# Causal scores and values in 64x64 quarters of TensorE's array, with the masked quarter left out

## The chip, the core and the metric

One core of a Trainium2 chip runs the whole program. A core has TensorE (PE, matmuls, which writes to the banks of PSUM), VectorE (DVE), ScalarE (ACT), GpSimd (POOL), and SyncE (SP), which here issues most loads. Each engine works through its own instructions in order and waits on semaphores for the others. The metric is the time of one execution on the device in microseconds (us); lower is better. Before the change it is 606.27 us, the median of three runs (605.86 to 606.37).

## What is computed

A retention layer (linear attention with a decay `gamma` for each head, causal), then a gated feed-forward layer without an activation, then a normalised one with SiLU. All of it is in float32:

```python
def _attn_ref(q, k, v):                       # 2 batches, 8 heads, 768 steps, 64 wide
    gamma = 1.0 - 2.0 ** (-5.0 - np.arange(H))
    for t in range(S):
        state = gamma * state + np.einsum('bhd,bhe->bhde', k[:, :, t], v[:, :, t])
        y[:, :, t] = scale * np.einsum('bhd,bhde->bhe', q[:, :, t], state)

x = y as 1536 tokens x 512
x = ((x @ w_a) * (x @ w_b)) @ w_out                       # 512 -> 1536 -> 512
xn = x / sqrt(mean(x * x) + 1e-6) * rms_g
out = (silu(xn @ w_gate) * (xn @ w_val)) @ w_out2         # 512 -> 1536 -> 512
```

## The kernel before

**Stages.** The retention layer fills the first 70 us, the two feed-forward layers the rest. The change is in the retention layer alone, which is worked in 12 chunks of 128 steps (6 per batch; chunk n and n + 2 are neighbours of one batch). The 8 heads of a chunk are 4 pairs `p` of 2 heads `r`; the 64 numbers of head `r` lie in the lower or upper 64 partitions. For every chunk there are four PE steps. `scores` (tile `sc`): keys times queries, 8 matmuls with 64 rows in, 128 out and 128 columns; DVE multiplies the two banks by the decayed causal mask, which gives `p`. `past` (tile `ya`, from `sd` and `qd`): queries times the state from earlier chunks, 8 matmuls of 64 by 64 and 128 columns, each in a quarter of the 128x128 array; chunks 0 and 1 have none. `values` (tile `ya`, from `p` and `k`): values times masked scores, 8 matmuls of 128 by 64 and 128 columns, added to the same banks. `state` (tile `st`, from `vd`): 8 matmuls of 128 by 64 and 64 columns; the last two chunks have none. In the trace each float32 matmul of the retention layer is two instructions, so a step of 8 matmuls is 16 rows.

**Around them.** `vd` (values times a decay) is made on DVE or POOL, `qd` (queries times a decay) on POOL or DVE, `sd` (the state) is copied out by ACT. After `values` ACT rounds the result to `xh`, DVE forms the rest `xl`, and ACT copies it once more to `xf` or `x`. The first products of the feed-forward layer (`c`, three passes with `xh`, `xl` and the weights `uh`, `ul`) are mixed in between the chunks. Loads go through SP: per chunk a queries-and-keys tile (512 KB, named `q`) and a keys-and-values tile (512 KB, named `k`), the mask (512 KB), weights (`raw`, 512 KB each).

**Order.** Nothing is issued in the order of the code. `Plan` records every operation; `dues` and `list` (lines 355 to 470) sort them with priced durations, and the table `SHIFTS` moves single operations earlier or later. The string `HEAD` (line 83) says in which order the steps of the retention stage are recorded: S scores, P past, V values, T state, `d` the decays, `m` the mask load, and `warm8` for 8 matmuls on zeros ahead of all. Every PE matmul goes through `mm` (line 536), which gives its price to the plan; every instruction is emitted by line 492, so the trace tells groups apart by tile names.

## Time and profile before

| what | value |
|---|---|
| median of three runs | 606.27 us |
| the profiled execution | 605.8 us, of which the profile's span is 604.0 us |
| PE busy | 595.6 us (99%) |
| DVE, ACT, POOL busy | 489.1 (81%), 422.4 (70%), 118.9 us (20%) |
| retention stage | from the first `sc` at 6.72 us to the first `y` at 69.77 us |
| granted clock of PE | 1.00 nearly throughout; 0.50 from 8.49 to 15.32 us |

A granted clock of 1.00 is 2.4 GHz, 0.50 is 1.2 GHz. A row of the timeline gives start and length of a run of alike instructions; the length reaches to the modelled end of the last one and so past the start of the next, because matmuls are pipelined. What a run costs the engine is therefore read from its start to the next run's start.

### The profile page before, as it was taken

The page shows a single profiled execution, that of the slowest core. Times are in us where ns is not written, and L with a number is a line of the kernel's source. Part 1 is how long each engine was busy: PE and PEld are TensorE (multiplying, and loading weights), DVE is VectorE, ACT ScalarE, POOL GpSimd, SP SyncE. Part 2 cuts the span into 40 slices and gives each one's busy share as a digit, 9 for nine tenths or more (in the row PEclk, how much of TensorE's full clock was granted, in tenths as well). Part 3 has the DMA queues.
Part 4 walks back from the last instruction along what each step waited for, and adds up shares of the span by engine and source line. Part 5 has one row for each costly group of instructions (what it writes and reads, how often), then busy time and mean ns, then how long its engine had stood idle before and what let it go on. Part 6 is the DMA issues. An engine that isn't in the chain of part 4 may idle for free.

```text
span 604.0 us, 9800 instructions
## 1 busy us (share of the span) xinstructions
PE 595.6 (99%) x3584; PEld 509.7 (84%) x3584; DVE 489.1 (81%) x886; ACT 422.4 (70%) x804; POOL 118.9 (20%) x135
## 2 busy tenths in 40 slices
PE   7999999999999999999999999999999999999997
PEld 6988888988888888888897888888888888888886
DVE  4799796695898996887789999598888898698554
ACT  5756787455888886778556977588687897787630
POOL 1330000013223323323100000002242323233210
PEclk7999999999999999999999999999999999999999
DMA  8884146018979988799941134335897897878875
GB/s 327 303 321 174 43 151 227 2 45 140 246 144 200 206 160 169 148 174 171 279 152 35 37 138 154 125 78 121 168 191 141 160 195 163 164 146 155 135 214 206
DMA packets 40352, 98.27 MB, mean 163 GB/s; under 512 B 4590, under 2 KB 4974, under 8 KB 40304
## 3 DMA queue, kind: packets, MB, share of 16 engines
q0 software_dynamic: 17312, 31.47, 35.4%
q1 hardware_dynamic: 22704, 66.07, 32.3%
q8 instruction: 28, 0.46, 0.3%
q10 hardware_dynamic: 288, 0.10, 0.1%
q14 instruction: 20, 0.16, 0.1%
HBM read 56.73 MB, written 40.89 MB: 162 GB/s over the span
## 4 chain that ended last, share of the span: by engine, by line
PE 91%; DMA 3%; issue 2%; DVE 2%; POOL 1%; ACT 0%; SPq 0%; POOLq 0%; DVEq 0%
PE b L492 30%; PE y L492 17%; PE d L492 16%; PE x_P L492 12%; PE c L492 11%; PE ya L492 2%; PE sc L492 2%; DMA q<-in_qk 1%; DMA acc<-out 1%; DMA out<-z 1%; PE st L492 1%; POOL out L492 1%; DVE vd L492 1%; PE ms L492 0%; PE rb L492 0%
## 5 line engine op out<-in xcount | busy, mean ns | idle before, releaser
L492 POOL DMA_DIRECT2D out<-z x60 | 52.4, 900 | 229.1 <-ACT z L492 197.9
L492 POOL DMA_DIRECT2D partial<-z x60 | 52.4, 926 | 204.9 <-ACT z L492 174.1
L492 PE MATMUL y<-h,o 128*128 128x512 f32 (+2 forms) x294 | 69.8, 389 | 1.2 <-DVE h L492 0.7
L492 PEld LDWEIGHTS y<-h,o 128*128 128x128 f32 x294 | 53.9, 188 | 13.2 <-DVE h L492 1.0
L492 ACT COPY z<-x_P 128x512 f32<-128x512 f32 x88 | 50.8, 589 | 18.3 <-PE x_P L492 16.6
L492 PE MATMUL b<-xh,uh 128*128 128x512 f32 x160 | 62.8, 392 | 0.0
L492 PE MATMUL b<-xl,uh 128*128 128x512 f32 x160 | 62.6, 391 | 0.0
L492 PE MATMUL b<-xh,ul 128*128 128x512 f32 x160 | 62.4, 390 | 0.0
L492 DVE TENSOR_TENSOR ul<-wt,uh 128x512 fp32r<-128x512 f32 x82 | 53.6, 686 | 6.1 <-ACT uh L492 6.0
L492 ACT CAST uh<-wt 128x512 fp32r<-128x512 f32 x82 | 48.3, 622 | 12.0 <-PE d L492 9.7
L492 ACT CAST v<-raw 128x512 f16<-128x512 bf16 x72 | 56.0, 791 | 0.5
L492 PE MATMUL x_P<-r,l 128*128 128x512 f32 x192 | 51.9, 391 | 0.0
L492 ACT ACTIVATE v<-raw 128x512 int32<-128x512 uint32 x72 | 48.2, 679 | 3.6 <-DMA raw<-in_w 3.6
L492 PE MATMUL y<-h,l 128*128 128x512 f32 x192 | 47.6, 390 | 0.0
L492 PE MATMUL b<-th,uh 128*128 128x512 f32 x120 | 47.2, 394 | 0.0
L492 PE MATMUL b<-tl,uh 128*128 128x512 f32 x120 | 47.1, 392 | 0.0
L492 PE MATMUL b<-th,ul 128*128 128x512 f32 x120 | 46.7, 389 | 0.0
L492 DVE TENSOR_TENSOR u<-u,b 128x512 f32<-128x512 f32 x40 | 27.4, 685 | 23.7 <-PE b L492 16.8
L492 ACT COPY z<-y 128x512 f32<-128x512 f32 x56 | 32.8, 587 | 18.8 <-PE y L492 16.9
L492 DVE TENSOR_TENSOR g<-g,d 128x256 f32<-128x256 f32 x80 | 33.3, 418 | 15.3 <-ACT g L492 7.9
L492 PE MATMUL d<-xh,ul 128*128 128x256 f32 x160 | 45.2, 283 | 0.0
L492 PE MATMUL d<-xl,uh 128*128 128x256 f32 x160 | 45.2, 283 | 0.0
(148 smaller groups left out, 1512.6 us busy)
## 6 DMA issues: line engine op xcount, KB each, us to landing
raw<-in_w SPq DMA_DIRECT2D x72, 512.0 KB, 4.8
partial<-z POOLq DMA_DIRECT2D x60, 256.0 KB, 5.3
out<-z POOLq DMA_DIRECT2D x60, 256.0 KB, 5.1
q<-in_qk SPq DMA_DIRECT2D x12, 512.0 KB, 6.7
k<-in_kv SPq DMA_DIRECT2D x10, 512.0 KB, 7.9
partial<-z SPq DMA_DIRECT2D x12, 256.0 KB, 2.1
acc<-partial SPq DMA_DIRECT2D x6, 512.0 KB, 6.8
out<-z SPq DMA_DIRECT2D x12, 256.0 KB, 2.8
```

What stands on the lines that cost most here:

```text
L492: getattr(self.engines[op.engine], method)(real(out), *map(real, args), **{k: real(a) for k, a in kwargs.items()})
```

## The change

Of a 128 x 128 block of scores the quarter of the later keys and the earlier queries is masked to zero. The new kernel does not compute it.

- **`scores`**: 16 matmuls instead of 8, each 64 rows by 64 outputs, in a quarter of the array: the earlier 64 keys against all 128 queries (128 columns), the later 64 keys against the later 64 queries (64 columns). For every second pair of heads the two key halves change places on the partitions (`turned`, on the host), so that of two pairs one fills each half of the bank with 128 columns and the other with 64. The bank holds 384 instead of 512 columns.
- **mask**: packed to the same 384 columns per bank; its load is 384 KB instead of 512 KB, and the DVE product `p` runs over 128x384 instead of 128x512.
- **`values`** is cut in two. A new step `early` takes the earlier queries: 8 matmuls of 64 by 64 and 64 columns. The rest takes the later queries: 8 matmuls of 128 by 64 and 64 columns.
- **marks**: `early` reads other rows of the array than `past` and adds to the same outputs. After `past` of each of the 10 chunks that have one, ACT copies 64x1 of the bank to `marks`, and one matmul of a single column reads that copy ahead of `early` (against the zero tile `warm`, into an unused column).
- `warm8` becomes `warm13`, the price in `mm` for a 64x64 matmul now grows with its columns, and `SHIFTS` holds other numbers, so the order of other work changes too.

```diff
-    6: -96050, 8: 11700, 17: 7750, 19: 24150, 22: 17850, 39: 18750, 40: 26200, 45: 18750, 58: -35200, 64: -17850, 95: 19200, 98: 26400, 113: 2800,
...
+    5: -64750, 6: -71600, 7: -68050, 19: 21550, 22: 20500, 30: 36800, 41: 16750, 45: 18750, 46: 15900, 62: -37200, 72: 5700, 76: 2000, 101: 20400,
...
-HEAD = "lq0 lw m lk0 warm8 S0 d L1 lq3 lq2 lk2 x c0 x x lw lk3 x W0 P0 V0 F0 x w1 S1 Q2 L4 x T0 lw lw P1 V1 F1 T1 x x Ha0 S2 P2 V2 F2 Q3 w2 c0 S3 x T2 W3 P3 x x V3 F3 x S4 x T3 L5 L6 D2 Q4 W4 L7 c1 Ua0 x Q5 W5 T4 x Hb0 Ub0 x D3 G0 S5 P4 V4 R0 F4 x L8 Q6 W6 x S6 T5 P5 V5 F5 c1 x L9 Q7 w7 x T6 S7 P6 V6 F6 x L10 D4 Q8 W8 P7 T7 V7 F7 S8 x x L11 q9 W9 x t0 t1 c1 x x Ua1 Ub1 G1 x x S9 P8 R1 x D5 T8 q10 V8 F8 x t1 c1 Ua2 x x Ub2 x G2 x R2 S10 P9 V9 F9 x q11 t1 T9 x Ua3 x x Ub3 G3 S11 x R3 T10 P10 P11 V10 F10 x x t1 V11 F11"
+HEAD = "lq0 lw m lk0 warm13 S0 d L1 lq3 lq2 lk2 x c0 x x lw lk3 x W0 P0 V0 F0 x w1 S1 Q2 L4 x T0 lw lw P1 V1 F1 T1 x x Ha0 S2 P2 V2 F2 Q3 w2 c0 S3 x T2 W3 P3 x x V3 F3 x S4 x T3 L5 L6 D2 Q4 W4 L7 c1 Ua0 x Q5 W5 T4 x Hb0 Ub0 x D3 G0 S5 P4 V4 R0 F4 x L8 Q6 W6 x S6 T5 P5 V5 F5 c1 x L9 Q7 w7 x T6 S7 P6 V6 F6 x L10 D4 Q8 W8 P7 T7 V7 F7 S8 x x L11 q9 W9 x t0 t1 c1 x x Ua1 Ub1 G1 x x S9 P8 R1 x D5 T8 q10 V8 F8 x t1 c1 Ua2 x x Ub2 x G2 x R2 S10 P9 V9 F9 x q11 t1 T9 x Ua3 x x Ub3 G3 S11 x R3 T10 P10 P11 V10 F10 x x t1 V11 F11"
...
-        n = out.shape[-1]
+        n = 1
+        for size in out.shape[1:]:
+            n *= size
...
-        each = 0.443 * n if n > HB else 123.6 if n == HB else 111 if full else 111 * (n + 8) / 136 if out.shape[0] == P or a[0].shape[0] == P else 54
+        each = 0.443 * n if n > HB else 123.6 if n == HB else 111 if full else 111 * (n + 8) / 136 if out.shape[0] == P or a[0].shape[0] == P else 54.6 * (n + 8) / 136
...
-            mask_sb = ac.tile([P, 2, NP, C], F32, name="mask_sb")
+            mask_sb = ac.tile([P, 2, NP // 2, 3, C // 2], F32, name="mask_sb")
+            warm = ac.tile([P, P], F32, name="warm")
...
-                p_t[n] = a2.tile([P, 2, NP, C], F32, tag="p", name=f"p{n}")
-                sc = [bank("Y", f"sc{n}_{r}").rearrange("p (n c) -> p n c", n=NP) for r in range(2)]
+                p_t[n] = a2.tile([P, 2, NP // 2, 3, C // 2], F32, tag="p", name=f"p{n}")
+                sc = [bank("Y", f"sc{n}_{r}")[:, :NP // 2 * 3 * C // 2].rearrange("p (e x c) -> p e x c", e=NP // 2, x=3) for r in range(2)]
                 plan.cut()
+                q, k = (qk_t[n][:, e].rearrange("p n (x c) -> p n x c", x=2) for e in range(2))
                 for p in range(NP):
-                    for r in range(2):
-                        h = slice(r * D, (r + 1) * D)
-                        mm(sc[r][:, p, :], qk_t[n][h, 1, p, :], qk_t[n][h, 0, p, :], start=True, stop=True)
+                    for first in (1, 0):
+                        for r in range(2):
+                            h = slice(r * D, (r + 1) * D)
+                            if first:
+                                to, x = p & 1, slice(0, 2 + (p & 1), 1 + (p & 1))
+                            else:
+                                to, x = 1 - (p & 1), slice(1 + (p & 1), 2 + (p & 1))
+                            mm(sc[r][to * D:(to + 1) * D, p // 2, x], k[h, p, 1 - first], q[h, p, 1 - first:], start=True, stop=True)
...
+            ya_all = {}
+            marks = ac.tile([P, LINE // 8], F32, name="marks")
+
             def past(n):
-                ya_t[n] = [bank(tag, f"ya{n}_{r}").rearrange("p (n c) -> p n c", n=NP)[:, :NP // 2] for r, tag in enumerate(("A", "AY"[n % 2]))]
+                ya_all[n] = [bank(tag, f"ya{n}_{r}") for r, tag in enumerate(("A", "AY"[n % 2]))]
+                ya_t[n] = [y.rearrange("p (n c) -> p n c", n=NP)[:, :NP // 2] for y in ya_all[n]]
...
+                    plan.cut()
+                    act.copy(marks[:D, n:n + 1], ya_t[n][1][:D, 1, C - 1:])
+
+            def early(n):
+                plan.cut()
+                if n >= B:
+                    mm(ya_all[n][0][:D, NP // 2 * C:NP // 2 * C + 1], warm[:D, :D], marks[:D, n:n + 1], start=False, stop=True, skip_group_check=True)
+                for p in range(NP):
+                    for r in range(2):
+                        to, e = place(p, r)
+                        h = slice((p & 1) * D, (1 + (p & 1)) * D)
+                        mm(ya_t[n][r][to, e, :C // 2], kv_t[n][h, 1, 2 * p + r, :], p_t[n][h, r, e, 0, :], start=(n < B), stop=True, skip_group_check=True)
 
             def values(n):
+                early(n)
                 j, o = n // CPT, (n % CPT) * C
                 if o == 0:
                     x_tiles(0, j)
                     if j < 2:
                         xf[j] = [held(place_of("sum", 2 * j + r), [P, 2, TB], F32, f"xf{j}_{r}") for r in range(2)]
-                y = ya_t.pop(n)
+                y = ya_t[n]
                 plan.cut()
                 for r in range(2):
                     for p in range(NP):
                         to, e = place(p, r)
-                        mm(y[r][to, e, :], kv_t[n][:, 1, 2 * p + r, :],
-                           p_t[n][:, r, p, :], start=(n < B), stop=True, skip_group_check=True)
+                        mm(y[r][to, e, C // 2:], kv_t[n][:, 1, 2 * p + r, :],
+                           p_t[n][:, r, e, 1 + (p & 1), :], start=(n < B), stop=True, skip_group_check=True)
...
+def turned(a, axis, heads):
+    a = a.copy()
+    for h in range(H):
+        if h // 2 % 2:
+            one = (slice(None),) * heads + (h,)
+            a[one] = a[one].take([*range(C // 2, C), *range(C // 2)], axis=axis - (heads < axis))
+    return a
...
-    mask = mask.reshape(NP, 2, C, C).transpose(2, 1, 0, 3).reshape(C, 2 * NP * C)
+    mask = turned(mask, 1, 0).reshape(NP // 2, 2, 2, C, 2, C // 2).transpose(3, 2, 0, 1, 4, 5)
+    mask = np.stack([np.concatenate([mask[r * C // 2:(r + 1) * C // 2, :, :, r, :1], mask[r * C // 2:(r + 1) * C // 2, :, :, :, 1]], axis=3) for r in range(2)])
+    mask = mask.reshape(C, 2 * (NP // 2) * 3 * (C // 2))
...
-    kv = np.stack([i[n].reshape(B, H, CPB, C, D).transpose(2, 0, 3, 1, 4).reshape(NCH, C, DM) for n in ("k", "v")], axis=2).reshape(NCH, C, 2 * DM)
+    kv = [i[n].reshape(B, H, CPB, C, D).transpose(2, 0, 3, 1, 4) for n in ("k", "v")]
+    kv = np.stack([turned(a, 2, 3).reshape(NCH, C, DM) for a in kv], axis=2).reshape(NCH, C, 2 * DM)
```

**PE, third and fourth chunk.** Before: the end of `past` of one chunk (tile `ya_0_290`), `values` of both, `st` and the next `sc`.

```order
L492 MATMUL ya_1_292<-qd_256,sd_237 64x128
L492 MATMUL ya_0_277<-p_270,k_221 64x128 x4
L492 MATMUL ya_1_279<-p_270,k_221 64x128 x4
L492 MATMUL ya_0_290<-p_287,k_239 64x128 x4
L492 MATMUL ya_1_292<-p_287,k_239 64x128 x4
L492 MATMUL st<-vd_309,k_221 64x64 x8
L492 MATMUL sc_0_340<-q_258 128x128
```

The same place after: the last two of `early` for the third chunk, `st`, the rest of its `values`, `st` of the next chunk, and the first `sc` of the fifth.

```order
L489 MATMUL ya_0_330<-p_325,k_176 64x64
L489 MATMUL ya_1_332<-p_325,k_176 64x64
L489 MATMUL st<-vd_327,k_176 64x64 x8
L489 MATMUL ya_0_330<-p_325,k_176 64x64 x4
L489 MATMUL ya_1_332<-p_325,k_176 64x64 x4
L489 MATMUL st<-vd_350,k_198 64x64 x8
L489 MATMUL sc_0_404<-q_216 64x128
L489 MATMUL sc_1_406<-q_216 64x128
L489 MATMUL sc_0_404<-q_216 64x64
L489 MATMUL sc_1_406<-q_216 64x64
```

What moved: the two `values` no longer stand together; each has 8 matmuls of `early` ahead of it, and the fourth chunk's comes behind the fifth chunk's scores.

**ACT, the same place.** After, with the two marks (`ya_1_332` and `ya_1_342` are the banks of the third and fourth chunk); PE's matmul on the first mark stands directly behind the fourth chunk's `past`.

```order
L489 COPY g_305<-c_0_0_266 128x256
L489 COPY marks<-ya_1_332 64x1
L489 COPY marks<-ya_1_342 64x1
L489 COPY sd_384<-st 128x256
L489 CAST xh_0_196<-ya_0_330 128x2x128
L489 ACTIVATE v_1_402<-raw_1_247 128x512
```

Before, the conversion of a weight (`v`) stood directly between `g` and the `xh` of the third chunk:

```order
L492 COPY g_254<-c_0_0_224 128x256
L492 ACTIVATE v_1_274<-raw_1_205 128x512
L492 CAST v_1_274<-raw_1_205 128x512
L492 CAST xh_0_172<-ya_0_277 128x2x128
L492 CAST xh_0_172<-ya_1_279 128x2x128
```

Here the marks and one copy of the state now come ahead of it, and the weight's conversion comes behind the first `xh`.

**SP, the first loads.** Before:

```order
L492 DMA raw_0_84<-in_w 128x1024
L492 DMA q_97<-in_qk 128x1024
L492 DMA mask_sb<-in_mask 128x1024
L492 DMA q_102<-in_qk 128x1024
L492 DMA k_104<-in_kv 128x1024
L492 DMA k_106<-in_kv 128x1024
L492 DMA q_108<-in_qk 128x1024
L492 DMA q_132<-in_qk 128x1024
L492 DMA raw_1_205<-in_w 128x1024
```

After:

```order
L489 DMA raw_0_84<-in_w 128x1024
L489 DMA q_102<-in_qk 128x1024
L489 DMA mask_sb<-in_mask 128x768
L489 DMA k_107<-in_kv 128x1024
L489 DMA q_109<-in_qk 128x1024
L489 DMA k_111<-in_kv 128x1024
L489 DMA q_113<-in_qk 128x1024
L489 DMA q_145<-in_qk 128x1024
L489 DMA k_176<-in_kv 128x1024
```

The first values tile now comes ahead of the second queries tile (on PE the first chunk's `values` now stands ahead of the second chunk's `sc`), and the second weight moved from the ninth to the twelfth load.

## Rows read from the trace of the kernel before

**Rows 1.** The page: the span, busy times, and the granted clock in 40 slices.

```profile
span 604.0 us, 9800 instructions
PE 595.6 (99%) x3584; PEld 509.7 (84%) x3584; DVE 489.1 (81%) x886; ACT 422.4 (70%) x804; POOL 118.9 (20%) x135
PEclk7999999999999999999999999999999999999999
```

**Rows 2.** Busy by stretch: PE, PEld, DVE, ACT, POOL; granted clock, DMA share, GB/s.

```profile
5.08:8.49 3.41, 1.76 (x18) 1.26 (x18) 1.54 (x3) 2.05 (x3) 0.00 (x0) 1.00 1.03 421
8.49:15.32 6.83, 6.47 (x58) 5.09 (x58) 4.85 (x8) 4.35 (x13) 1.85 (x2) 0.50 1.02 411
32.40:36.00 3.60, 2.84 (x62) 2.19 (x50) 3.60 (x6) 1.46 (x5) 2.98 (x2) 1.00 0.92 328
17.97:69.77 51.80, 51.04 (x717) 44.29 (x716) 45.26 (x76) 31.35 (x77) 8.76 (x7) 1.00 0.57 211
```

**Rows 3.** Timeline of PE at the start: start, length, run, [idle before, releaser].

```profile
1.06 3.78 PE L492 MATMUL w<-warm 128*128 128x128 f32 x16 [1.06 <-DVE small L492]
6.72 1.16 PE L492 MATMUL sc<-q 64*128 64x128 f32 x16 [1.88 <-DMA q<-in_qk]
7.82 1.43 PE L492 MATMUL decays<-tables 2*128 2x512 f32 x2
9.30 2.08 PE L492 MATMUL sc<-q 64*128 64x128 f32 x16
```

**Rows 4.** Timeline of DVE and POOL at the start: who waits for which load.

```profile
8.06 1.29 DVE L492 TENSOR_TENSOR p<-sc,mask_sb 128x512 f32<-128x512 f32 x2 [0.46 <-DMA mask_sb<-in_mask]
11.95 1.04 POOL L492 TENSOR_TENSOR vd<-k,dg_sb 128x512 f32<-128x512 f32 x1 [9.97 <-DMA k<-in_kv]
14.51 2.52 POOL L492 TENSOR_TENSOR qd<-q,dq_sb 128x512 f32<-128x512 f32 x2 [1.52 <-DMA q<-in_qk]
```

**Rows 5.** Timeline of PE, retention steps of later chunks, at full clock.

```profile
17.97 2.06 PE L492 MATMUL sc<-q 64*128 64x128 f32 x32
19.95 1.10 PE L492 MATMUL ya<-qd,sd 64*64 64x128 f32 x32
20.99 1.97 PE L492 MATMUL ya<-p,k 128*64 128x128 f32 x32
22.79 0.63 PE L492 MATMUL st<-vd,k 128*64 128x64 f32 x16
23.35 1.16 PE L492 MATMUL sc<-q 64*128 64x128 f32 x16
24.44 0.69 PE L492 MATMUL st<-vd,k 128*64 128x64 f32 x16
...
40.74 0.64 PE L492 MATMUL st<-vd,k 128*64 128x64 f32 x16
41.21 1.05 PE L492 MATMUL ya<-p,k 128*64 128x128 f32 x16
...
48.47 0.67 PE L492 MATMUL ya<-qd,sd 64*64 64x128 f32 x16
49.06 0.69 PE L492 MATMUL st<-vd,k 128*64 128x64 f32 x16
```

**Rows 6.** Timeline of DVE and PE around 35 us.

```profile
32.55 1.77 DVE L492 TENSOR_TENSOR vd<-k,dg_sb 128x512 f32<-128x512 f32 x1
34.98 0.66 PE L492 MATMUL ya<-p,k 128*64 128x128 f32 x8 [0.41 <-DVE p L492]
```

**Rows 7.** DVE groups from 17.97 to 69.77 us: count, busy, mean ns, idle before.

```profile
L492 DVE TENSOR_TENSOR p<-sc,mask_sb 128x512 f32<-128x512 f32 x20 | 13.0, 682 | 3.2 <-PE sc L492 3.2
L492 DVE TENSOR_TENSOR xl<-ya,xh 128x256 fp32r<-128x256 f32 x18 | 7.1, 414 | 0.8 <-ACT xh L492 0.8
```

**Rows 8.** Timeline of ACT: an operation on 128x2, and one step of the conversion of a weight.

```profile
2.47 0.20 ACT L492 ACTIVATE small<-small 128x2 f32<-128x2 f32 x1
...
19.05 0.77 ACT L492 CAST v<-raw 128x512 f16<-128x512 bf16 x1
```

More of the change, by code (lines that the diff above doesn't have):

```diff
@@ L1508, in gated @@
                 cast(0, *FIRST[i], g_t[i])
-            warm = ac.tile([P, P], F32, name="warm")
             vec.memset(warm, 0.0)
@@ L1517, in masks @@
             def masks(_):
-                dma("sp", mask_sb.rearrange("p r n c -> p (r n c)"), mask)
+                dma("sp", mask_sb.rearrange("p r e x c -> p (r e x c)"), mask)
             def decays(_):
@@ L1634, in _consts @@
     mask = np.where(apart >= 0, scale * g[:, None, None] ** np.maximum(apart, 0), 0)
-    mask = mask.reshape(NP, 2, C, C).transpose(2, 1, 0, 3).reshape(C, 2 * NP * C)
+    mask = turned(mask, 1, 0).reshape(NP // 2, 2, 2, C, 2, C // 2).transpose(3, 2, 0, 1, 4, 5)
+    mask = np.stack([np.concatenate([mask[r * C // 2:(r + 1) * C // 2, :, :, r, :1], mask[r * C // 2:(r + 1) * C // 2, :, :, :, 1]], axis=3) for r in range(2)])
+    mask = mask.reshape(C, 2 * (NP // 2) * 3 * (C // 2))
     c = np.arange(CPB)[:, None] * C
-    dk = g ** (S // 2 - (c + t)[:, :, None]).transpose(1, 0, 2)
+    dk = turned(g ** (S // 2 - (c + t)[:, :, None]).transpose(1, 0, 2), 0, 2)
     gq = np.repeat((g ** (c - C)).reshape(CPB, NP, 2, 1), D, axis=3).reshape(CPB, NP, P).transpose(2, 0, 1)
```

25 rows, old and new, of the table SHIFTS are left out of this document.

## The prediction

> **What bounds the kernel now.** I read the busy shares first: PE is busy for 595.6 of 604.0 us, DVE for 81%, the others for less [rows 1]. So time is lost or won on PE, and only in the retention stage, since nothing else is rewritten. There, from 17.97 to 69.77 us, PE is busy for 51.04 of 51.80 us and DVE for 45.26 [rows 2]: PE is the bound, DVE close behind. Before 17.97 us it is otherwise. PE starts its first scores at 6.72 us, after 1.88 us without work [rows 3]. Loads land one after the other: first queries 6.72, mask 8.06, second queries 9.30, the second values tile is waited for until 11.95, later queries until 14.51 [rows 3, 4], which is about 1.3 us for each 512 KB. And from 8.49 to 15.32 us PE is granted a clock of 0.50, the lower level of 1.2 GHz, after a stretch in which it was busy for 1.76 of 3.41 us [rows 2].
>
> **Prices of the PE steps**, at full clock, from start to start [rows 5]. Two chunks of scores take 19.95 - 17.97 = 1.98 us, one chunk 24.44 - 23.35 = 1.09: a chunk costs 0.89, coming from another array shape 0.20. `past`: two chunks 20.99 - 19.95 = 1.04, one chunk 49.06 - 48.47 = 0.59: 0.45 and 0.14 to 0.16. `values`: 22.79 - 20.99 = 1.80 for two, 0.90 each. `state`, which has the shape of `values` and half its columns, stands between two `values` from 40.74 to 41.21: 0.47. So on 128x64 half the columns cost half. And `past` shows that 64x64 matmuls with 128 columns run four at a time, at half the price of 128x64 (0.45 against 0.90).
>
> **Part 1, scores.** 8 matmuls of 128 columns in quarters, as `past`: 0.45. 8 more with 64 columns: 0.23 if a quarter also takes half the time for half the columns, 0.45 if it does not. I take 0.23, nearest to the 0.47 of `state`. New price 0.68, gain 0.89 - 0.68 = 0.21 a chunk; other bound -0.01, no gain.
>
> **Part 2, values.** The later queries have the shape of `state`: 0.47. `early`, 8 matmuls of 64x64 and 64 columns: 0.23, bound 0.45. Sum 0.70 (0.92), gain 0.20 (bound -0.02). For the 10 chunks behind 17.97 us both parts give 10 x 0.41 = 4.1 us, or nothing.
>
> **Part 3, changes of shape.** Behind 17.97 us there are now 7 stretches of 64x128, 6 of 64x64, 7 of 128x64 and 4 of full arrays; by the order after the change 10 of 64x64, 9 of 128x64 and 6 full. At 0.20, 0.16, 0.20 (`state` alone lasts 0.69 from 24.44 on, less 0.47 [rows 5]) and 0.19 for full arrays, an estimate from the other three, that is 1.4 + 0.96 + 1.4 + 0.76 = 4.5 us before and 1.6 + 1.8 + 1.14 = 4.5 after. Zero.
>
> **Part 4, marks.** Ten matmuls of one column, two instructions each, stand ahead of `early`. No row shows one; the smallest step of 16 costs 0.47, so 0.03 an instruction, and because the next matmul of that quarter waits for both I take 0.1 us, 1.0 in all. Each also waits for an ACT copy of 64x1, and all of PE is queued behind it. The smallest ACT operation took 0.20 us [rows 8]. In two places (chunks 2 and 6, counted from 0) only one `past` of 0.45 us lies between the copied result and the mark; result, copy and signal need more, so some 0.3 us of waiting each, 0.6 together. In the other eight, scores, `values` or `y` lie between, at least 0.7 us, which hide a copy unless ACT has other work ahead of it. Sum +1.6 us; bounds +0.3 (waits hidden) and +9 (rival 3).
>
> **Part 5, DVE.** The 20 products `p` from 17.97 on take 682 ns for 512 columns, `xl` 414 for 256 [rows 7]; 384 should take 548, so DVE loses 20 x 0.134 = 2.7 us of its 45.26. PE's stretch shrinks by as much as 3, so DVE's share stays where it is, near 88%, and waits for it stay possible. Now there is one: around 35 us PE waits for a `p` that stood behind a `vd` of 1.77 us, which ran beside POOL's `qd` [rows 6]; in that stretch PE was idle for 0.76 of 3.60 us [rows 2]. DVE has other neighbours in the new order; I take half of it back, -0.4 us (bounds -0.8 and +1.2), and +0.5 for new waits on DVE (0 to +1.5). ACT's ten copies, 2 us on an engine busy for 31.35 of 51.80 [rows 2], cost only through the marks.
>
> **Part 6, the start.** The mask is 128 KB smaller: a quarter of 1.3 us, it lands near 7.7 instead of 8.06. Then come first values (9.0), second queries (10.3), second values (11.6), later queries (12.9, 14.2). The order after: first scores 6.72 to 7.5, decays, `p` from 7.75 to 8.8, first values 9.0 to 10.0, second scores 10.3 to 11.1, `state`, `p`, second values 12.3 to 13.2, `state`, and `c` from about 14.2, once `xh` is there, to 15.8. Before, the stage of third scores began at 17.97: gain 2.2 us. This holds at full clock. The clock fell behind the stretch from 5.08 to 8.49, of which PE was idle for 1.65 us, and stayed at 1.00 across 0.76 us of idle time around 35 us [rows 2]. Sixteen instructions on zeros took 3.78 us with their tail [rows 3]; ten more take 2.4 at that pace and 1.2 at double the clock, and so fill most of the 1.88 us ahead of the first scores. Later idle times in my list are 0.9 us at most. So I take the full clock. At 0.50 the same list ends near 17.5: gain 0.5.
>
> **The sum.** -2.2 (start) - 4.1 (scores, values) + 1.6 (marks) - 0.4 + 0.5 (DVE) = -4.6 us, from the profiled execution's 605.8 (span 604.0, 1.8 around it): 601.2. The median of the three runs is 0.47 above that execution, so the forecast is 606.27 - 4.6, rounded to **601.6 us**. What PE gains stays, because in the rest PE has at most 8.4 - 1.1 - 1.9 - 0.8 = 4.6 us without work [rows 1 to 3], and DVE, at 81% over the whole span, catches up there.
>
> **Rivals.**
>
> 1. *The quarter brings nothing on PE.* No row shows 64x64 matmuls above 16 in 0.45 us, 28 ns each; `state` too needs 0.47 for 16 [rows 5]. If instructions and not columns set this, parts 1 and 2 give zero: -1.7 (start, as the shorter steps count there too) + 1.6 - 0.4 + 0 = -0.5, 605.8 us. For it: both numbers per instruction are equal. Against it: `state` has two matmuls at a time and `past` four, so the equality can be chance. The Trainium skill states this rule ("TensorEngine Tiling (Array Packing)", Instruction Overhead): a matmul of few columns lasts as long as one of about 60, so no tiling factor should come out of a dimension that is small already; 64 columns is just at that mark. By this rule the time would be the 605.8 of this rival; the rows bear it out only so far as the two equal numbers do.
>
> 2. *`early` runs two at a time.* In `past` and scores a row half of the array always writes the same bank; in `early` both row halves write both banks at the same time. No row shows that. If the halves must take turns, `early` costs 0.45 instead of 0.23: 12 x 0.22 = 2.6, which gives 604.3 us. The Trainium skill says so ("TensorEngine Tiling (Array Packing)", Gotcha 1: PSUM Pressure): different row tiles cannot access the same PSUM bank at the same time. By it the time would be 604.3; no run so far bears on it.
>
> 3. *The marks cost more than the quarter brings.* ACT works in order, and one step of the conversion of a weight takes 0.77 us [rows 8]. If every mark's copy comes late, by 0.9 us in the mean, ten marks cost 9 + 1 instead of 1.6: -4.6 + 8.4 = +3.8, **610.1 us**. It decides from about 0.6 us per mark on, where 6.2 us of marks eat up the other gains. For it: a `past` followed by a mark empties PE, and everything on PE stands behind. Against it: only two marks follow so closely, and in the order at the third chunk ACT has both marks in a row behind an old copy `g`.
>
> The low clock at the start adds 1.7 to any of these; within the forecast that is 603.3.
>
> **Chances.** Forecast with either clock 0.48; rival 1 0.18; rival 2 0.13; rival 3 0.13; better than 599, with the waits at 35 us gone and marks for nothing, 0.08. The range takes in rivals 1 and 2 with the low end of the forecast: full clock, no waits (-2.2 - 4.1 + 0.3 - 0.8 = -6.8) gives 599.5, and 0.5 for the rest of the order, 599.0; the top is rival 1 at 605.8, and 0.3 above it. What is left out is rival 3 and part of the last case. A difference of 0.2% (1.2 us) is about what a measurement of this kernel can tell from none: faster 0.48 + 0.13 + 0.08 + 0.01 = 0.70, same 0.17, slower 0.13.
>
> **What would show it.** In the timeline after: a chunk's scores 0.68 us from start to start with 32 instructions (0.89 for rival 1), `early` 0.23 (0.45 for rivals 1 and 2), `values` behind it 0.47; waits of PE for ACT `marks` under 1 us in total (rival 3: over 5); `p` at 548 ns; granted clock 1.00 from 5 us on and third scores near 16 us; the first `y` behind the last retention step near 65 us. The forecast is wrong if the clock falls again, if PE's waits for DVE grow beyond 1.5 us, or if feed-forward work on PE gets longer by its new order.

## The result and the profile after

The changed kernel takes **610.2 us** (607.2 to 612.7), the kernel before beside it 605.8: a ratio of 1.0074, 95% interval 1.0056 to 1.0091. It is slower; the prediction was 601.6 us with a range that ended at 606.1. The executions of the changed kernel lie further apart than those of the kernel before (604.5 to 607.1); that the waits shown below fall out differently from one to the next would explain it, but only one execution of each kernel was profiled, so this is not shown. The profiled one is 2.1 us above the median.

The page of the profiled execution (612.27 us), to be read against [rows 1], has the span, busy time, granted clock in 40 slices, and the queue that brings instructions (packets, MB).

```profile
span 610.5 us, 10614 instructions
PE 594.5 (97%) x3998; PEld 509.1 (83%) x3998; DVE 484.7 (79%) x886; ACT 419.2 (69%) x814; POOL 117.9 (19%) x135
PEclk9998999999999999999998999999999999999999
q8 instruction: 31, 0.51, 0.3%
```

PE works 1.1 us less than before and the span is 6.5 us longer, so the time went into standing still. What was forecast for the start came true. Two runs of PE's timeline: the warm-up and the third and fourth chunks' scores; then the group of DVE's products `p` in the retention stage.

```profile
1.06 4.59 PE L489 MATMUL w<-warm 128*128 128x128 f32 x26 [1.06 <-DVE small L489]
...
15.34 1.57 PE L489 MATMUL sc<-q 64*64 64x128 f32 x64
```

```profile
L489 DVE TENSOR_TENSOR p<-sc,mask_sb 128x384 f32<-128x384 f32 x20 | 10.5, 550 | 2.6 <-PE sc L489 2.5
```

That stage begins at 15.34 us instead of 17.97 [rows 5], at full clock, and `p` takes 550 ns (548 was worked out). What went wrong stands in PE's waits: who it waited for, us in total, times, longest.

```profile
PE st L489 <- issue: 4.9, 2, 3.5
PE ya L489 <- issue: 2.1, 1, 2.1
...
PE c L489 <- DVE ul L489: 0.8, 1, 0.8
PE ya L489 <- POOL qd L489: 0.6, 1, 0.6
```

"Issue" is time for which no semaphore accounts. It is three waits, each in the middle of a step whose first matmuls had already run, so the data were there. PE's timeline (start, length, run, [idle before, releaser]):

```profile
20.07 0.33 PE L489 MATMUL st<-vd,k 128*64 128x64 f32 x2
21.88 0.68 PE L489 MATMUL st<-vd,k 128*64 128x64 f32 x14 [1.48 <-issue]
...
36.32 0.71 PE L489 MATMUL ya<-qd,sd 64*64 64x128 f32 x17
39.10 0.56 PE L489 MATMUL ya<-qd,sd 64*64 64x128 f32 x12 [2.08 <-issue]
...
42.21 0.57 PE L489 MATMUL st<-vd,k 128*64 128x64 f32 x13
46.24 0.48 PE L489 MATMUL st<-vd,k 128*64 128x64 f32 x3 [3.46 <-issue]
```

From the last matmul ahead of a wait to the first behind it that is 1.70 + 2.34 + 3.68 = 7.7 us. During the third, the clock falls. Stretches of the changed kernel (busy time of PE, PEld, DVE, ACT, POOL; granted clock, DMA share, GB/s):

```profile
4.07:45.03 40.96, 32.07 (x841) 28.25 (x840) 25.77 (x48) 22.69 (x69) 12.36 (x10) 1.00 0.85 324
42.60:46.20 3.60, 0.19 (x7) 0.05 (x1) 0.75 (x2) 0.25 (x1) 0.00 (x0) 0.84 0.18 71
45.03:51.86 6.83, 5.62 (x15) 4.44 (x16) 4.36 (x6) 2.29 (x5) 0.00 (x0) 0.50 0.21 64
324.92:328.34 3.42, 3.09 (x7) 2.48 (x8) 3.42 (x10) 0.82 (x2) 0.00 (x0) 0.50 0.00 0
```

The clock held at 1.00 across the first two waits. In the stretch around the third, PE worked for 0.19 of 3.60 us; from 45.03 us on, still inside the wait, the clock was 0.50 (1.2 GHz) for 6.8 us. It was 0.50 once more from 324.92 us on, 1.4 us behind the end of a wait of 1.0 us for DVE at the join of the two feed-forward parts.

**Reading the waits.** Count PE's instructions in the trace from the start of the program, its semaphore instructions with its matmuls and weight loads: PE pauses exactly behind instructions 704, 1472 and 1728, and all three are 192 more than a multiple of 256. Queue q8 moved 0.51 MB in 31 packets, 16 KB each: one for every 256 of PE's 8033 instructions (in the kernel before, 28 packets for 7202). Between the second and the third wait PE uses up 256 instructions in 3.5 us. The DMA queues from 39.1 to 43.9 us, and in the following 1.0 us (packets, MB, share of 16 engines):

```profile
q1 hardware_dynamic: 328, 1.16, 68.8%
q14 instruction: 1, 0.01, 0.7%
```

```profile
q8 instruction: 1, 0.02, 5.6%
q1 hardware_dynamic: 5, 0.00, 1.2%
```

From 39.1 to 43.9 us queue q1 moves 1.16 MB of loads and q8 nothing; at 43.95, when the loads have thinned out, q8's packet runs for 0.9 us, and PE goes on at 46.24. The same order holds at the second wait (packet at 36.77 us, PE at 39.10) and the first (19.53, 21.88). So the theory to test, **A**: PE's instructions come in pieces of 256, one piece ahead, over the engines that carry the loads; in a stage that uses a piece in 3.5 to 4.5 us while loads run, a piece comes too late. The rival, **B**: the quarters themselves make PE stop (64x64 tiles, marks, packed products).

### The profile page after: what moved, and what is told of

Read it like the earlier page. It is cut to its first block, busy times and chain, and to the rows that moved or that the text cites. A ratio compares the mean times of both kernels' runs of the same rounds, so it can differ in the third digit from the quotient of the medians.

```text
span 610.5 us, 10614 instructions
## 1 busy us (share of the span) xinstructions
PE 594.5 (97%) x3998; PEld 509.1 (83%) x3998; DVE 484.7 (79%) x886; ACT 419.2 (69%) x814; POOL 117.9 (19%) x135
## 4 chain that ended last, share of the span: by engine, by line
PE 94%; DMA 2%; issue 1%; DVE 1%; POOL 0%; ACT 0%; SPq 0%; POOLq 0%
PE b L489 31%; PE y L489 18%; PE d L489 16%; PE x_P L489 13%; PE c L489 11%; PE ya L489 2%; DMA q<-in_qk 2%; PE sc L489 1%; PE st L489 1%; PE rb L489 0%; POOL qd L489 0%; DVE acc L489 0%; DVE xl L489 0%; DVE ul L489 0%; PE ms L489 0%
## 5 line engine op out<-in xcount | busy, mean ns | idle before, releaser
L489 PE MATMUL d<-xh,uh 128*128 128x256 f32 x160 | 45.3, 283 | 0.2 <-DVE g L489 0.2
L489 PE MATMUL d<-t,uh 128*128 128x256 f32 x240 | 45.2, 282 | 0.0
```

Source lines behind the costliest of these rows:

```text
L489: getattr(self.engines[op.engine], method)(real(out), *map(real, args), **{k: real(a) for k, a in kwargs.items()})
```

## The start alone

The kernel before with 13 instead of 8 warm-up products, order kept:

```
- HEAD = "lq0 lw m lk0 warm8 S0 d ...
+ HEAD = "lq0 lw m lk0 warm13 S0 d ...
```

> The kernel before with 13 warm-up matmuls instead of 8, order the same: the start alone. If the longer warm-up is what keeps the clock up at the start: granted clock 1.00 from 8.5 to 15.3 us, third scores at 16 to 17.2 instead of 17.97, time 0.7 to 2 us below before. If the start is bound by its loads: same time within 0.5 us.

Measured: 603.25 us, ratio 0.9957 (0.9943 to 0.9972). Of that kernel, the stretch that answers to the first two of [rows 2]:

```profile
5.18:15.08 9.90, 9.05 (x119) 7.30 (x118) 6.30 (x12) 7.86 (x22) 1.94 (x2) 1.00 1.03 414
```

The clock stays at 1.00 and the third chunk's scores start at 15.08 us, with the whole mask and no quarters. This one edit gives 2.6 us; it beats both the kernel before and the changed one, and no other kernel of this study has a lower ratio (the intervals of three overlap with its own).

## Where the waits stand: three runs

**64 instructions ahead of everything.** In the changed kernel, 16 matmuls of one column follow the warm-up:

```
+ for i in range(16):
+     ...
+     plan.group.calls.append(("matmul", w[c, :1], (warm[r, :D], warm[r, :1]), ...))
```

> The changed kernel with 64 more PE instructions (16 one-column matmuls on zeros) behind the warm-up, in the idle time ahead of the first scores; every engine's order is otherwise the same. Theory A (PE runs out of instructions: they arrive in pieces of 256, and a piece comes too late where 256 are used up quickly while loads run): the long waits that no semaphore explains come again at the same numbers of PE instructions (704, 1472, 1728), which is 64 instructions earlier in the program: not in the state matmuls of the fourth and eighth chunk and the past of the eighth, but near the state step of the third chunk, in scores of the eighth chunk and in values of the eighth chunk. Sum of these waits 4 to 9 us, time 608 to 613. Theory B (the waits belong to their places: a mark, a state copy or a semaphore that the profile does not show): they stay at the same matmuls.

Measured: 606.5 us, ratio 1.0017 (1.0002 to 1.0032). Its timeline of PE:

```profile
16.22 0.39 PE L489 MATMUL c<-xh,uh 128*128 128x256 f32 x1 [1.68 <-issue]
...
39.55 0.45 PE L489 MATMUL sc<-q 64*64 64x128 f32 x10 [2.16 <-issue]
43.67 0.94 PE L489 MATMUL ya<-p,k 64*64 64x64 f32 x19 [0.52 <-issue]
```

These waits are in a `c`, in scores and in `values`, where the changed kernel has none; a fourth is in a `state` step, of an earlier chunk than there. By count they are behind instructions 448, 704, 1472 and 1728, and together they are 7.1 us. They are tied to the number of the instruction, not to the work. The time was expected higher (608 to 613 us): with the last wait at 0.74 instead of 3.68 us the clock did not fall there.

**The kernel before, with nearly as many instructions.** 16 matmuls of one column in every `past`, 64 instructions a chunk, no quarters and no marks:

```
+ for i in range(16):
+     ...
+     plan.group.calls.append(("matmul", full[r][to, NP // 2 * C:NP // 2 * C + 1], (warm[h, :D], warm[h, :1]), ...))
```

> The kernel before, with 16 one-column matmuls on zeros added to each of the ten past steps, into unused columns (64 more PE instructions a chunk, 640 in all, three quarters of what the change adds); order the same, no quarters in scores and values. Theory A: waits that no semaphore explains appear on PE between 17 and 50 us, 1 us or more in sum, and the time is 3 to 9 us above before, more than the 16 matmuls themselves take (0.2 to 0.45 us a chunk, 2 to 4.5 in all). Theory B and every theory that blames the new quarters or the marks: no such waits; only the 2 to 4.5 us.

Measured: 611.8 us, ratio 1.0105 (1.008 to 1.013).

```profile
41.06 0.56 PE L492 MATMUL ya<-warm 64*64 64x1 f32 x25 [0.56 <-issue]
...
47.31 0.76 PE L492 MATMUL ya<-p,k 128*64 128x128 f32 x10 [1.82 <-issue]
```

These are waits that the kernel before does not have, behind instructions 1216 and 1472, 0.76 and 2.10 us from start to start; the added matmuls themselves take 0.44 to 0.52 us a chunk. B falls as the sole cause: with scores and values whole and no marks, added instructions alone make the same waits.

**The loads.** Both edits are made in the changed kernel. In the first, two weight loads (the third and fourth, issued at 31.67 us) are cut from 512 to 8 KB, so that the rest of these weights is left out; in the second, the same two loads have their full size but are issued ahead of the load `q8` (the ninth chunk's queries and keys, not the DMA queue of that name), 7.0 us earlier:

```
- dma("sp", t.rearrange("p n t -> p (n t)"), src)
+ plan.record("sp", "dma_start", t.rearrange("p n t -> p (n t)")[:, :16], (src[:, :16],), ...)
```

```
- SP: ... q7, q8, raw1_0, raw1_1, q9, ...
+ SP: ... q7, raw1_0, raw1_1, q8, q9, ...
```

> The changed kernel, same order on every engine, but the two weight loads (512 KB each) that are issued at 31.7 us are cut to 8 KB; the products of the second weight block use the first block's values, so part of the computation is changed. Theory A, with the fetch of instructions queued behind data loads: less is queued ahead of the fetch that is asked for near 33 us, the wait of 2.1 us near 36.8 goes to under 0.7, the later one (3.5 us at 42.6) stays or shrinks; time 2 to 6 us below the changed kernel, 604 to 608. If the fetch is slow by itself, whatever the loads: waits as before within 0.5 us, time 609 to 611. Theory B: no difference, since nothing waits for these two loads until 46 us.

> The changed kernel, with two weight loads of 512 KB moved ahead of the load of q8 in SP's queue: they are issued at about 25 us, where the DMA rings have room, instead of at 31.7 us just ahead of the fetch that PE asks for at 33.1 us. The instructions of PE, ACT, DVE and POOL keep their order. Theory A with the part that a fetch waits for the loads queued ahead of it: the wait at instruction 1472 (2.34 us) falls to 0 to 1.5 us, the one at 1728 (3.68 us) falls too, since the first loads after it come sooner, and the time is 604 to 608. If a fetch does not wait for the loads but has a delay of its own, nothing moves: 2.3 and 3.7 us again, 609 to 611. The fetch asked for at about 29 us may come later, for the loads now lie ahead of it; PE needs it only at 33 us.

Measured: 606.1 us with small loads (ratio 1.0004, 0.9985 to 1.0022), 608.4 with earlier loads (1.0056, 1.0035 to 1.0078; 605.2 to 611.4). With small loads the three waits are 1.64, 1.70 and 2.85 us instead of 1.70, 2.34 and 3.68, and one of 0.67 is added: smaller, but not as small as expected. The loads behind moved up (the next weight load went out at 37.65 instead of 49.17 us), which would explain that. Behind the last of them the clock stayed at 1.00 (from 44.36 to 52 us), unlike the changed kernel's: of the 4.8 us between the two profiled executions, the shorter waits make 0.9 and the `c` at the full clock 2.4. With earlier loads, in the profiled execution, which at 605.2 us was the fastest of eight, the wait behind 1472 is under 0.4 and that behind 1728 is 1.21 us; but PE began the piece ahead of instruction 1216 at 27.9 us, with the two loads already issued, the packet came at 30.89, and PE stood for 1.61 us behind 1216, where it had not stood. In the changed kernel the same packet came 0.9 us after PE had begun that piece, here 3.0. A fetch that comes after the loads ahead of it fits both runs; a fetch with a delay of its own, whatever the loads, does not fit the second. A cure it is not: the loads have to run at some time, and there is a fetch at every time.

## How much is the order, how much the quarters

The change also brought a new order for all later steps. Theory **C**: part of the loss is that order, above all at the join (305 to 345 us). Each engine's order, of the one kernel, was given to the other, and two kernels took the new order up to the first norm and the old one from there.

```
- total, start, seq = self.order()
+ seq = [self.ops[int(i)] for i in ORDER.split()]      # every engine in the other kernel's order
```

> The kernel before with 13 warm-up products, no quarter and no mark, but with every engine and queue in the order of the changed kernel. Theory C: the join costs 2.3 us more than in the kernel before, from the new order alone, so 603.25 + 2.3 to 4 = 605.5 to 607; no wait for instructions over 0.3 us, since 128 a chunk are executed. If the join's loss comes from the quarters or from the waits ahead of it: 603 to 604.

> The changed kernel whole, but every engine and queue works in the order of the kernel before; what was added stands where it must: `early` right ahead of the later values, each mark's copy right behind its `past`. It separates the new order of all steps (the changed table of shifts) from the quarters. Theory C (a second cost beside the instruction supply: the new order makes PE wait and its clock fall at the join of the two feed-forward parts, 305 to 345 us, where it loses 3.9 us instead of 1.6): there the loss is 1.6 us again and the granted clock stays 1.00; in the retention stage the waits for instructions remain, 4 to 8 us together, since the count of instructions is the same. Time 604 to 608. If the order costs nothing: 609 to 611.

> The kernel before with 13 warm-up products and no quarters, in the new order up to the first norm at the join of the two feed-forward parts, in the old order behind it. Theory C (the new order loses at the join, 4.3 us instead of 1.6 between 300 and 345 us, and gains about 1.4 us ahead of it): 604.46 - 2.4 = 602.0, so 601.3 to 602.8. If the loss at the join follows from what lies ahead of it and not from the order there: 604 to 605.

> The changed kernel whole in its own order up to the first norm at the join, and in the old order behind it. Theory C: the join's loss goes back to 1.6 us and the granted clock stays 1.00 there, while the waits for instructions in the retention stage remain as in the changed kernel, since nothing ahead of 300 us is moved: 610.2 - 2.5 = 607.7, so 606 to 609. If the join costs nothing in the changed kernel: 610 again.

Measured: without quarters in the new order 604.5 us (ratio 0.9967, 0.9953 to 0.9982); the changed kernel in the old order 610.5 (1.0078, 1.0056 to 1.0099), with waits behind 448, 704, 1472 and 1728; the two mixed orders 604.65 (0.9981, 0.997 to 0.9992) without quarters and 609.4 (1.0055, 1.0039 to 1.007) with them. All four missed the times that theory C expected. Without quarters the new order costs some 0.1% (0.9967 against 0.9957 in the old order, with intervals that overlap), where 2.3 us or more were expected, and mixing did not help: waits at the join come in either form. The low clock there is the order's all the same: the run without quarters has it in the new order too (0.75 from 315 to 320 us), and the changed kernel with the old order at the join has not (1.00 from 300 to 345 us). First without quarters in the new order, then in the mixed order:

```profile
PE ms L578 <- DVE acc L578: 1.0, 1, 1.0
```

```profile
PE y L578 <- DVE acc L578: 0.8, 1, 0.8
PE d L578 <- ACT g L578: 0.8, 1, 0.8
PE y L578 <- DVE h L578: 0.7, 1, 0.7
```

So theory C explains little of the time, and what an order at the join would have to look like stays open. The run without quarters in the new order is worth more as a ruler: step by step it does what the changed kernel does, in the same sequence. PE's timeline for the fifth to seventh chunks there, without quarters:

```profile
28.02 1.16 PE L578 MATMUL sc<-q 64*128 64x128 f32 x16
29.11 0.67 PE L578 MATMUL ya<-qd,sd 64*64 64x128 f32 x16
29.71 1.16 PE L578 MATMUL sc<-q 64*128 64x128 f32 x16
30.80 0.67 PE L578 MATMUL ya<-qd,sd 64*64 64x128 f32 x16
31.40 1.10 PE L578 MATMUL ya<-p,k 128*64 128x128 f32 x16
32.33 0.63 PE L578 MATMUL st<-vd,k 128*64 128x64 f32 x16
32.79 1.05 PE L578 MATMUL ya<-p,k 128*64 128x128 f32 x16
33.67 0.63 PE L578 MATMUL st<-vd,k 128*64 128x64 f32 x16
34.23 1.16 PE L578 MATMUL sc<-q 64*128 64x128 f32 x16
```

and of the changed kernel (the runs of marks and `early` left out but for the first mark of each chunk):

```profile
30.24 0.90 PE L489 MATMUL sc<-q 64*64 64x128 f32 x32
30.96 0.62 PE L489 MATMUL ya<-qd,sd 64*64 64x128 f32 x16
31.40 0.85 PE L489 MATMUL sc<-q 64*64 64x128 f32 x32
32.07 0.62 PE L489 MATMUL ya<-qd,sd 64*64 64x128 f32 x16
32.51 0.16 PE L489 MATMUL ya<-marks,warm 64*64 64x1 f32 x1
...
33.46 0.64 PE L489 MATMUL st<-vd,k 128*64 128x64 f32 x16
34.03 0.21 PE L489 MATMUL ya<-marks,warm 64*64 64x1 f32 x1
...
35.03 0.64 PE L489 MATMUL st<-vd,k 128*64 128x64 f32 x16
35.60 0.90 PE L489 MATMUL sc<-q 64*64 64x128 f32 x32
```

From start to start: scores 1.09 before, 0.72 and 0.67 now; `past` 0.60 and 0.44; mark and values 0.93 and 0.88 before, 0.95 and 1.00 now; `state` 0.46 and 0.56, now 0.57 twice. The piece of two chunks takes 6.21 and 5.36 us: 0.42 a chunk saved, all of it by the scores and by `past`, which now has neighbours of its own array shape (0.45 was its price without a change of shape). The values in quarters save nothing.

The whole account, from the third chunk's scores to the first `y`: 48.24 us without quarters (15.89 to 64.13), 56.68 with them (15.34 to 72.02), 8.4 more. Waits for instructions make +7.7; 24 `c` at the low clock +2.4 (8.08 instead of 5.69); waits for DVE and POOL +1.4 (0.8 and 0.6). That leaves, by subtraction, -3.1 for the steps themselves, which is what was forecast for them (10 x 0.31). The stage is compared within one order only, because an order shifts work across its end: without quarters it lasts 52.10 us in the old order (15.08 to 67.18) and 48.24 in the new one, and the new order is not the faster of the two.

## Parts of the change by themselves

**Values alone.** Scores, mask and `p` as before, values in quarters: in all chunks, in the first six, in the last six (new order), and in all and the last six (old order).

```
- mm(sc[r][to * D:(to + 1) * D, p // 2, x], k[h, p, 1 - first], q[h, p, 1 - first:], ...)
+ mm(sc[r][:, p, :], qk_t[n][h, 1, p, :], qk_t[n][h, 0, p, :], ...)
...
+ QUARTERS = range(NCH)     # or range(6), or range(6, NCH)
```

> The values alone in quarters: the changed kernel with its scores, products with the mask and mask as they were before (eight full 64x128 scores a chunk, unpacked mask), everything else as changed, in the changed kernel's order. PE executes about 164 instructions a chunk instead of 196 (128 before). Theory A (PE stands because its instructions come in pieces of 256 over the same DMA rings as the loads, and pieces are used up faster than they come): the same three places in the instruction count, later in the program because fewer instructions lie ahead, and shorter waits, 0 to 4 us together instead of 7.7. Without any wait the time would be 605.8 - 2.6 (start of the clock) - 2.0 (ten chunks of values at 0.2 us less) = 601.2, so 601 to 605. Rival B (the 64x64 tiles themselves, two in one bank, make PE stop): the tiles of the values are all still there, so waits of 6 us and more stay and the time is 607 to 610.

> As the run with the values alone in quarters, but only in the first six of the twelve chunks; the other six take their values in eight products of the full height, as before. Theory A: from 30 us on, where loads run and chunks follow each other closely, PE needs as few instructions as before, so no wait over 0.5 us there; up to 1.5 us at instruction 704 ahead of it. Time 605.8 - 2.6 - 1.0 = 602.2 without a wait, so 602 to 604. Rival B: waits in the first six chunks alone, about as the first one of the changed kernel (1.7 us) and more, 604 to 606.

> As the run with the values alone in quarters, but only in the last six chunks; the first six as before. Theory A: the wait at instruction 704 (1.7 us in the changed kernel) is gone, since no instructions were added ahead of it; from 30 us on 36 more a chunk leave 0 to 3 us of waits. Time 605.8 - 2.6 - 1.2 = 602.0 without a wait, so 602 to 605. Rival B: the waits at 36 and 42 us stay at 5 us together, 606 to 608.

> Values alone in quarters in all chunks (scores, mask and products with it as before), in the order of the kernel before. With the join as in the kernel before, theory C expects the 603.25 us of the kernel before with 13 warm-up products, less 2.0 us (ten chunks of values at 0.20 us less), plus 0.5 to 2.5 us of waits for instructions: 601.5 to 604. If the order costs nothing, it is 606.5 us, as with the values alone in quarters in the new order.

> Values alone in quarters in the last six chunks, in the order of the kernel before. Theory C: 603.25 us less 1.2 us, plus 0 to 1 us of waits for instructions, 602 to 603. If the order costs nothing: 605.8 us, as in the new order.

Measured, in this sequence: 606.5 us (1.0012, 1.0004 to 1.0021), 608.2 (1.0046, 1.0033 to 1.0059), 605.8 (1.0004, 0.9995 to 1.0013), 605.5 (0.9996, 0.9985 to 1.0007), 606.1 (1.0003, 0.9993 to 1.0014). The waits shrank as theory A says: at 164 instructions a chunk they are 0.95, 1.33 and 0 us in the new order, 0.8 and 0.7 in the old one, against 7.7 at 196, and B would have kept them. They stand at a piece's end each time, but three of the four behind 1216, which is none of the three places expected; with the first six chunks none over 0.5 us was expected from 30 us on, and the one of 1.33 us is at 37.7 us. Theory A did not say which of the fetches comes late. Every time was above the range that theory A or C gave it, by 0.8 to 4.2 us. All of these counted on a gain of 0.20 us a chunk that is not there: a chunk of values takes 1.00 us instead of 0.93, `state` behind it 0.57 instead of 0.46 to 0.56. In the old order marks add 0.8 us (three waits for ACT). Of the 608.2 us with the first six chunks, up to 2.4 us stay unexplained (608.2 less the wait of 1.3 and the 604.5 of the new order without quarters).

**Which rule slows the values?** The kernel before with 13 warm-up products, in its own order and with its scores, has the values alone in quarters, and the key halves are exchanged for every odd head instead of every second pair. In `early` a row half of the array then writes one bank, as in `past`, and no mark is needed. Against the values in quarters above:

```
- h = slice((p & 1) * D, (1 + (p & 1)) * D)
+ h = slice(r * D, (r + 1) * D)
```

> The kernel before with 13 warm-up products, in its own order, with the values alone in quarters, but with the key halves exchanged for every odd head instead of every second pair of heads: in `early` a row half of the array now writes one bank only, as in `past`, and no mark is needed. 32 instructions a chunk are added (160 instead of 128). If `early` was slow because both row halves wrote both banks (rival 2), it takes 0.23 us now and a chunk's values 0.70 to 0.75 instead of 0.92: 603.25 - 2.0 + 0 to 1 of waits for instructions = 601 to 602.5. If 28 ns an instruction is the limit (rival 1), `early` stays at 0.43 and the time is 603.5 to 605.5.

Measured: 603.1 us, ratio 0.9968 (0.9957 to 0.9979), no wait for instructions; in the profiled execution the clock was 0.50 from 11 to 14 us, which cost 1.2 us of it. Its values for one chunk, `early` and the later queries in one run:

```profile
30.73 1.03 PE L578 MATMUL ya<-p,k 64*64 64x64 f32 x32
31.59 0.63 PE L578 MATMUL st<-vd,k 128*64 128x64 f32 x15
```

The chunk takes 0.86 us from start to start: less than the 0.95 and 1.00 with marks and shared banks, and far from the 0.70 to 0.75 that would show the banks as the brake. Its `early` takes 0.34 of that, not the 0.43 expected of a limit of 28 ns an instruction, and not 0.23 either. An estimate is 0.23 for the columns and the rest for the change to 128x64 behind it; no run takes these apart.

**Scores alone, and both.** The kernel before with 13 warm-up products and its own order takes its scores in quarters from the third chunk on; zeros are written where the quarter is left out. A second run has the same scores in the mixed order of above. A third has the first one's scores and the values by odd heads: no marks, no packed products, 196 instructions a chunk.

```
- mm(sc[r][:, p, :], qk_t[n][h, 1, p, :], qk_t[n][h, 0, p, :], ...)
+ for a in range(2):
+     ...
+     mm(sc[r][half, p, a * D:], qk_t[n][h, 1, p, half], qk_t[n][h, 0, p, a * D:], ...)
...
+ mm(sc[r][D:, :, :D], warm[h, :D // 2].bitcast(BF16), warm[h, :P].bitcast(BF16), ...)
```

> The kernel before with 13 warm-up products, in its own order, with the scores alone in quarters from the third chunk on; the quarter that is left out is filled with zeros by one cheap bf16 product for each bank, since the unpacked products with the mask read it. Values, mask and DVE's work as before, no mark. 36 instructions a chunk are added. The scores of one chunk, 1.09 us with the change of shape before, should take 0.72 as in the changed kernel and 0.1 for the zeros; ten chunks gain 2.5 us: 603.25 - 2.5 + 0 to 1 of waits for instructions = 600.7 to 602. If the scores' gain in the changed kernel was only the other neighbours' (shapes), 602.5 to 604.

> The same order, and the scores alone in quarters from the third chunk on, with zeros filled in (164 instructions a chunk). In the old order the scores gave back on waits (0.8 us for instructions, 0.5 for DVE) most of their 2.4 us; if that is chance of the order, the gain shows here: 602.0 - 1.5 to 2.5 = 599.5 to 600.5. If the instruction supply takes it back again: 601 to 603.

> Both together: scores in quarters with zeros filled in, values in quarters by odd heads, no marks, order of the kernel before; 196 instructions a chunk, as many as in the changed kernel. Without waits for instructions 603.25 - 2.5 - 2.0 = 598.8. If the supply of instructions limits the stage as in the changed kernel, waits of 3 to 8 us and a fall of the clock come back, 602 to 607; if the waits had another cause in the changed kernel (marks, packed products), 599 to 600.

Measured: scores alone 603.4 us (0.9974, 0.9963 to 0.9985); in the mixed order 605.1 (0.9988, 0.9972 to 1.0003), with waits for instructions of 1.7 us; both 607.7 (1.0043, 1.0023 to 1.0064). With the zeros a single chunk's scores take 0.84 to 1.17 us instead of 1.09, less of a gain than the 0.72 and 0.67 of the changed kernel. In the first of these runs ten chunks of scores take 9.3 us against 10.3 in the run of the start alone, and waits for instructions, 0.8 us there and 1.7 in the second run, take it back. Of the run with both, PE's waits:

```profile
PE sc L578 <- issue: 3.6, 2, 2.1
```

They lie behind instructions 704 and 1472 again. With the marks and the packed products gone but the count back at 196, the long waits are back. With the added matmuls above, which make them without quarters, that settles A against B.

## Why the prediction was wrong

- **The step that failed** is the pricing of added matmuls in parts 1, 2 and 4: by columns and array shape alone. Each of them also brings a weight load, and the instructions of a chunk go from 128 to 196. That they must be delivered stood nowhere, which put this at nothing, and no row of before shows a wait for it: from one piece's end to the next, 256 instructions last 6.5 us and more there. In the profiled execution it costs 7.7 us, and the low clock from the third wait on another 2.4. "What PE gains stays" failed with it. One of the forecast's own signs of being wrong came with it, the fall of the clock, but in the middle of the stage and not at the start, where it was looked for. The three rivals did not contain the cause; that rival 3 has 610.1 us, next to the measured 610.2, is chance, because its mechanism did not happen: in the changed kernel's trace PE nowhere waits for a mark's copy.
- **Part 6** held in its size: third scores at 15.34 us (15.8 expected), 2.6 us instead of 2.2, full clock. It is the longer warm-up's alone: the kernel before with that one edit has them at 15.08 us, so the smaller mask and the quarters, which the part also counts, are not seen in the gain.
- **Parts 1 to 3** held as a sum and not one by one: in the piece of two chunks 0.42 us a chunk with the mark included, 0.31 forecast. Scores with `past` gained 0.55 and not 0.21; values gained nothing and not 0.20. That changes of shape went away at the one and came back at the other fits their prices, but is argued. That the changes balance was at most right over the whole.
- **Rivals 1 and 2** are out as they stood: the scores gain, so 28 ns an instruction is no floor, and shared banks with their marks cost at most 0.14 us a chunk (0.95 and 1.00 against 0.86), where rival 2 needs 0.22. The Trainium skill's two rules ("TensorEngine Tiling (Array Packing)", Instruction Overhead and Gotcha 1: PSUM Pressure) would have put the loss on the array; the traces put it on the supply.
- **Part 4**: in this order PE does not wait for marks (0.6 us forecast); the 1.0 us for their matmuls cannot be read apart from the values. **Part 5**: `p` is as worked out, the wait at 35 us is gone, and a new wait for DVE of 0.8 us lies within its range; the 0.6 us for POOL stood in no part.
- **Feed-forward work**, named as what would make the forecast wrong, did lose: the clock was low for 3.4 us at the join. The run without quarters has this too and bounds it, at 0.1% net for the new order.
- **The sum**: 606.27 - 4.6 is 601.67, rounded to 601.6; this changes nothing.

The page "Runtime: NRT & Kernel Launch" of the Trainium skill (section Instruction fetch mechanics) says that each engine's instructions are refilled in blocks of 16 KiB, 256 instructions, and that crossing a block is "mostly hidden". The block size agrees with the 256 between the waits here; that it is hidden does not hold in stretches that use a block in 3.5 to 4.5 us while transfers take 0.7 to all of the DMA engines' time.

## What to carry to other kernels

Count instructions beside array time: where PE's steps are cut into small tiles while loads fill the DMA engines, see how long 256 instructions last against how late the instruction queue's packet comes, and look in the waits for "issue" in mid-run. A split that saves columns but doubles matmuls is worth trying only where that time has room, and each part of it should be timed alone, as here the start was worth 2.6 us, the scores little and the values nothing. A change of array shape is better counted at the step that causes it than balanced over a stage.

## What the runs showed of the hardware

- All pauses of PE of over 1 us from start to start that no semaphore or load explains lie at 192 more than a multiple of 256 of its instructions (matmuls, weight loads and semaphore instructions), in eleven of these kernels, with different work at that place.
- A packet of 256 instructions takes 0.9 to 1.4 us in the first 70 us. In the changed kernel it starts 0.9 to 1.3 us after PE's first instruction of the piece ahead where the loads moved at most 0.4 MB in between, and 2.5 to 4.9 us after it where they moved 1.0 to 1.6 MB. Out of a pause PE goes on 1.2 to 1.5 us after the packet has landed.
- The granted clock of the changed kernel stayed at 1.00 across pauses of 1.7 and 2.3 us and went to 0.50 during one of 3.7 us; with small loads it stayed at 1.00 across one of 2.85 us; in the old order it was 0.60 from 22 to 25 us already, behind pauses of 1.1 and 2.1 us.
- 64x64 matmuls of 64 columns run below 28 ns each: 32 instructions of scores, half of them 64 columns wide, take 0.67 us, 21 ns each.
